# A four-batch attention and MLP kernel: group 0 of the last layer moved behind the pair, its first product in seven half products

## The chip, the cores and the metric

The program runs on one core of one Trainium2 chip. The metric is the device time of one execution in microseconds (us). Engines are named as in the profile: PE (TensorE matmuls; PEld its weight loads), DVE (VectorE), ACT (ScalarE), POOL (GpSimd), SP (SyncE, which issues most DMAs).

## The reference

```python
def _attn_ref(q, k, v, tau):                    # q, k, v: 4 batches, 8 heads, 576 tokens, 64
    scores = scale * np.matmul(q, k.transpose(0, 1, 3, 2))
    thresh = np.max(scores, axis=-1, keepdims=True) - tau
    scores = np.where(scores >= thresh, scores, -1000000000.0)
    ...                                         # softmax, then attn @ v
def _moe_ref(x, w_in, w_out):                   # x: 2304 x 512, w_in: 512 x 2048, w_out: 2048 x 512
    h = x @ w_in
    g = np.where(h >= 1, h, np.where(h <= -1, 0.0, (h + 1) ** 2 / 4))
    return g @ w_out
def _moe2_ref(x, w_in, w_out):                  # the same sizes
    h = x @ w_in
    g = h * np.clip(h + 3.0, 0.0, 6.0) / 6.0
    return g @ w_out
```

The output is `_moe2_ref` of `_moe_ref` of the attention's output. The change lies in the second MLP, called layer two here.

## The kernel before

Every number is kept as a high and a low part (fp32r), so that a product of two numbers is three matmuls: high by high, high by low, low by high. The 2304 tokens stand in five groups: groups 0 to 3 are the first 512 tokens of each batch, group 4 the 256 tokens that are left of all four. The hidden size of 2048 is 16 blocks `f` of 128.

Layer two runs in three stages. **Plain groups** (`dense`, called on L1497 with `order3` = groups 3, 4, 0): for each `f` the first product (`em_h`, L716, 12 matmuls; line L725), the gate (ACT Relu L738, DVE L739), its high part (ACT `gh`, L742) and low part (POOL `gl`, L743), and two steps later the second product (`em_out`, 12 matmuls of 512 columns, L767). **The pair** (`unit`, L1344): groups 1 and 2 together, the first product by seven block products in place of eight (Strassen-Winograd over two halves of the contraction, two blocks `f` and the two groups). For each of the 8 pairs `p` of blocks there are seven products of 6 matmuls with 512 columns (L1362), copies of partial sums on ACT (L1383), sums on DVE (`C`, L1388), four gates (L1147, L1148), and group 1's second product for the pair of blocks before (`outs_of`, L1157; matmuls L1165). Group 2's gated values go to DRAM (`rr`). **The end** (L1420 on): group 2's second product by seven for eight, in matmuls of 256 columns (`out_product`, L1287; L1300), with its inputs loaded from `rr`, summed on DVE and split on ACT, POOL and DVE.

The products by seven need sums of weights. `combine` (L1457) makes those of w_in out of the split weights, on DVE (`ex` L1473, `ws`, `wz`), from the second plain group on; they go to DRAM (`sd`) and come back as `sw` (`fetch`, L1129). `weight_sums` (L1172) makes those of w_out beside the pair (`te`, `ts`, `tz`); they go to `td` and come back as `tw`. `prepare` (L1098) makes the sums of tokens for the pair beside the last plain group.

While group 3 runs, the weights of layer two are still being split (`split_a`, `split_b`, L118 to L152): per weight tile two ACT passes, three DVE passes on `w_c` (L133, L136, L142), a POOL add (L144), the high part on ACT (L146) and the low part on POOL (L148). There are two `w_c` buffers. `ahead3` (L1485) calls this for each step. Each engine runs its queue in order; the order of the queues is fixed when the program is built.

Of the kernel before, what the change touches and what calls it, by code (L numbers as in the profile page):

```python
# [18 lines left out]
def kernel(  # L19
# [50 lines left out]
    td = [dram.tile([128, 2, 2, 512], F32R, name=f"td{p}") for p in range(KF // 2)]  # L70
    rd2 = [dram.tile([128, MAIN], F32, name=f"rr{f}") for f in range(KF)]
    xd, x2p, x2d = ([dram.tile([128, KD, n], F32, name=f"{nm}{w}") for w, n in enumerate(WIDE)]
# [67 lines left out]
    def split_b(kind, m, f):  # L140
# [6 lines left out]
        after(x, pins["S"])  # L147
        x = G.tensor_tensor(out=lo, in0=f32(c), in1=f32(hi), op=ALU.subtract)  # L148
# [918 lines left out]
    order3 = [NB - 1, NB, 0]  # L1067
# [30 lines left out]
    def prepare(step):  # L1098

        for c in range(2):  # L1100
# [6 lines left out]
            if step == 1:  # L1107
                part(0, c, b11)
                minus(t1, b12, b11)
            elif step == 2:  # L1110
                part(1, c, b21)
                minus(t2, b22, t1)
                minus(b12, b22, b12)
            elif step == 3:
                part(2, c, t2)
                minus(b11, t2, b21)
            elif step == 4:
                part(3, c, b12)
                part(4, c, b11)
            elif step == 5:  # L1120
                part(5, c, t1)
            elif step == 6:
                part(6, c, b22)

# [47 lines left out]
    def weight_sums():  # L1172

        for p in range(KF // 2):
            ex = []
            for f in (2 * p, 2 * p + 1):
                hi, lo = wsp["o", 1, f]
                t = wide["x"].tile([128, 512], F32, tag="xh3", name="te", bufs=2)
# [4 lines left out]
            s, u = (wide["x"].tile([128, 512], F32, tag="xl3", name="ts", bufs=2) for _ in range(2))  # L1183
            minus(s[:, 0:256], b12, b11)
            minus(s[:, 256:512], b22, s[:, 0:256])
            yield
            minus(u[:, 0:256], b22, b12)
            minus(u[:, 256:512], s[:, 256:512], b21)
            yield
            zs = []  # L1190
            for t in (s, u):
                z = stage.tile([128, 2, 512], F32R, tag="w_raw", name="tz", bufs=RAW)
                paced(S.activation(out=z[:, 0, :], in_=t, func=ACTF.Copy), "S")
                zs.append((t, z))
            yield
            for n, (t, z) in enumerate(zs):
                minus(z[:, 1, :], t, f32(z[:, 0, :]))
                nc.sync.dma_start(out=f32(td[p])[:, n], in_=f32(z))
                yield

    tw = {}

    def fetch_sum(n):

        p, x = divmod(n, 4)
        if p < 3:
            t = wide["x"].tile([128, 512], F32R, tag=RING[len(ring) % 6], name="tw", bufs=2)
            ring.append(t)
        else:
            t = place_of((n - 12) // 2, "hl"[n % 2], F32R, "tw")  # L1210
# [5 lines left out]
    def load_pair(p):  # L1216

        if p in (0, 2):
            rr[p] = [wide["p"].tile([128, MAIN], F32, tag="xst", name="r2", bufs=3) for _ in range(2)]
        elif p in (1, 3):  # L1220
            rr[p] = [wide["p"].tile([128, MAIN], F32, tag="xst", name="r2", bufs=3),
                     wide["t"].tile([128, MAIN], F32, tag="t0", name="r2")]
# [4 lines left out]
        for t, f in zip(rr[p], (2 * p, 2 * p + 1)):  # L1227
            nc.sync.dma_start(out=t, in_=rd2[f])
# [15 lines left out]
    def high_pair(p):  # L1244

        if p % 3 == 0:
            d = [[wide["x"].tile([128, 512], F32R, tag=tag, name="gt", bufs=2) for _ in range(2)]
                 for tag in ("xh3", "xl3")]
# [3 lines left out]
        elif p % 3 == 1:  # L1252
            d = [halves(f, "gt") for f in range(10, 14)]
        else:
            d = [(ringed("gh", F32R), ringed("gl", F32R)) for _ in range(4)]
        d[0] = [t[:, 0:256] for t in d[0]]
# [30 lines left out]
    def out_product(p, k, behind=None):  # L1287
# [5 lines left out]
        else:  # L1293
            n = {5: 0, 2: 1, 3: 2, 4: 3}[k]
# [14 lines left out]
    def out_sums(k):  # L1309
# [7 lines left out]
        def result(i, n, x, y, sign=1.0):  # L1317
            o = wide["p"].tile([128, 512], F32, tag="io", name="ob", bufs=3)
            scaled(o, x, y, sign)
            for m, q in enumerate((nc.sync, nc.scalar)):  # L1320
                q.dma_start(out=rows_of(G2, 2 * i + m)[:, n * 256:n * 256 + 256], in_=o[:, m * 256:m * 256 + 256])
# [22 lines left out]
    def unit():  # L1344

        accs, gg = {}, {}
        sums_of = weight_sums()
        last_p = KF // 2 - 1
        for p in range(KF // 2):

            def product(k, role, first=True):
# [4 lines left out]
                if first:  # L1356
                    banks[role] = bank(f"Q{(p + role) % 4}")
                y = 0
                for c in range(2):
                    xh, xl = combos[c, x]  # L1360
                    for l, r in ((0, xh), (0, xl), (1, xh)):
# [3 lines left out]
                        if p == last_p:  # L1365
                            after(mm, pins["T"])
                        pins["T"] = mm
                if p < last_p:
                    fetch(p + 1, w)
                    next(sums_of, 0)  # L1370
                else:
                    if k:
                        fetch_sum(4 + k)
                    {1: sum_pair, 2: high_pair, 3: low_pair}.get(k, lambda _: 0)(0)
                    if k == 3:
                        load_pair(2)
                return banks[role]

            banks = {}

            def copy(name, x):
                t = wide["p"].tile([128, MAIN], F32, tag="pb", name=name, bufs=KD)
                S.activation(out=t, in_=x, func=ACTF.Copy)  # L1383
                return t

            def add(name, x, y, op=ALU.add):
                t = place_of(14 + (name[2] == "2"), "hl"[name[1] == "2"], F32, name)
                V.tensor_tensor(out=t, in0=x, in1=y, op=op)  # L1388
                return t

            def outs(i):
                if p:
                    for f in (2 * p - 2, 2 * p - 1):
                        outs_of(G1, accs, i, f, gg[f], pins["T"] if p == last_p else None)

            def store(r, f):
                nc.sync.dma_start(out=rd2[f], in_=r)

            if p == last_p:
# [128 lines left out]
```

## Time and profile before

| | us |
|---|---|
| median of 3 runs | 1100.63 (1100.17 to 1101.37) |
| the profiled execution, its own time | 1102.58 |
| its span, first to last instruction | 1100.8 |
| PE busy | 1067.0 (97%) |
| DVE, ACT, POOL busy | 740.7, 656.6, 454.0 |

PE's granted clock was 0.992 on average. Matmuls are pipelined, so the time of one is longer than the distance from its start to the next one's start; the distance is what a matmul costs in a full stream. Layer two's plain groups run from about 710 us, the pair from about 930 us, the end from about 1046 us.

### The profile page before, as it was taken

Reading aid. Unit: us, or ns where it says so; the run is one execution under the profiler, and the core shown is the slowest. Engines: PE = TensorE matmul, PEld = TensorE weight load, DVE = VectorE, ACT = ScalarE, POOL = GpSimd, SP = SyncE. Lnnn points to the kernel's source line nnn. Section 1 sums busy time; section 2 is a strip of 40 time slices with the busy share of each in tenths; the row PEclk is TensorE's granted clock in tenths of the full one; section 3 lists DMA queues with packets and bytes.
Section 4 is the critical chain, followed back from the end, with each engine's and each line's share of the span. In section 5 each row is a group of like instructions: output and inputs, shape, how many; then the busy total and the mean of one; then the engine's idle time right before and its main releaser. Section 6 shows DMA issues by size and latency. Waiting matters only on the chain.

```text
span 1100.8 us, 18826 instructions
## 1 busy us (share of the span) xinstructions
PE 1067.0 (97%) x6658; PEld 882.2 (80%) x6658; DVE 740.7 (67%) x1432; ACT 656.6 (60%) x1304; POOL 454.0 (41%) x390
## 2 busy tenths in 40 slices
PE   7988889999999999999999999999999999999998
PEld 5555567777888888888889888888898888888888
DVE  5899887976676757256536755458565655778766
ACT  5777887776766767465556666645544333544542
POOL 0233667742222322146636665567723222211242
PEclk9999889999999999999999999999999999999999
DMA  6454446233222221015323555655244412877891
GB/s 170 117 98 101 117 118 149 64 75 88 70 66 66 45 61 44 30 50 172 94 73 125 164 178 164 212 169 154 77 154 151 136 58 67 269 259 250 279 348 39
DMA packets 178190, 140.97 MB, mean 128 GB/s; under 512 B 103088, under 2 KB 144304, under 8 KB 178096
## 3 DMA queue, kind: packets, MB, share of 16 engines
q1 hardware_dynamic: 176176, 138.95, 43.3%
q8 instruction: 52, 0.85, 0.3%
q10 hardware_dynamic: 1920, 0.82, 0.3%
q14 instruction: 42, 0.34, 0.1%
HBM read 93.00 MB, written 46.73 MB: 127 GB/s over the span
## 4 chain that ended last, share of the span: by engine, by line
PE 83%; DVE 8%; DMA 3%; ACT 2%; issue 1%; POOL 1%; SPq 1%; DVEq 0%; ACTq 0%; POOLq 0%
PE Q L725 27%; PE P L767 20%; PE Q L787 7%; PE Q L1362 6%; PE Q L482 6%; PE P L381 5%; PE Q L295 4%; PE P L1165 3%; DVE p L396 3%; DVE p L418 2%; PE P L1300 2%; PE Q L1300 1%; DMA tw<-td 1%; DVE xl L706 1%; SPq L234 1%
## 5 line engine op out<-in xcount | busy, mean ns | idle before, releaser
L743 POOL TENSOR_TENSOR gl<-r,gh 128x256 fp32r<-128x256 f32 (+1 forms) x158 | 167.1, 1058 | 324.6 <-ACT gh L742 312.2
L725 PE MATMUL Q<-xh,wih 128*128 128x256 f32 (+1 forms) x632 | 211.8, 335 | 2.6 <-DVE r L736 2.3
L725 PE MATMUL Q<-xl,wih 128*128 128x256 f32 (+1 forms) x632 | 207.3, 328 | 0.0
L725 PE MATMUL Q<-xh,wil 128*128 128x256 f32 (+1 forms) x632 | 207.2, 328 | 0.0
L736 DVE SCALAR_TENSOR_TENSOR r<-r,Q 128x256 f32<-128x256 f32 (+1 forms) x110 | 54.8, 498 | 124.6 <-ACT r L735 120.8
L418 DVE SCALAR_TENSOR_TENSOR p<-p,th,e 128x576 f32<-128x576 f32 x144 | 127.7, 909 | 15.8 <-ACT e L409 10.0
L725 PEld LDWEIGHTS Q<-xh,wih 128*128 128x128 f32 x632 | 120.1, 190 | 21.0 <-DVE r L736 4.1
L742 ACT ACTIVATE gh<-r 128x256 fp32r<-128x256 f32 (+1 forms) x158 | 79.6, 504 | 86.6 <-DVE r L736 31.1
L409 ACT ACTIVATE e<-p,nm 128x576 f32<-128x576 f32 x144 | 109.4, 775 | 36.2 <-DVE p L396 35.3
L725 PEld LDWEIGHTS Q<-xl,wih 128*128 128x128 f32 x632 | 120.2, 190 | 10.9
L725 PEld LDWEIGHTS Q<-xh,wil 128*128 128x128 f32 x632 | 120.1, 190 | 10.3
L295 PE MATMUL Q<-ident,p 128*128 128x128 f32 x656 | 107.3, 281 | 12.8 <-ACT Gf L446 9.7
L295 PEld LDWEIGHTS Q<-ident,p 128*128 128x128 f32 x656 | 74.0, 141 | 42.4 <-ACT Gf L446 16.1
L144 POOL TENSOR_TENSOR w_c<-w_c,w_raw 128x512 int32<-128x512 int32 x64 | 89.5, 1399 | 39.9 <-DVE w_c L142 20.6
L381 PE MATMUL P<-kt,qt 64*128 64x288 f32 (+2 forms) x508 | 82.8, 412 | 10.1 <-DVE p L396 8.1
L446 ACT ACTIVATE Gf<-Q 128x512 f32<-128x512 f32 x128 | 74.2, 595 | 15.8 <-PE Q L295 15.1
L1362 PE MATMUL Q<-xw,sw 128*128 128x512 f32 x336 | 81.0, 390 | 0.0
L396 DVE TENSOR_SCALAR_CACHE_REDUCE p<-P 128x576 f32<-128x576 f32 x90 | 65.2, 751 | 18.9 <-PE Q L295 11.9
L734 ACT ACTIVATE r<-Q,half 128x256 f32<-128x256 f32 (+1 forms) x110 | 58.5, 534 | 32.2 <-PE Q L725 25.3
L787 PE MATMUL Q<-gh,woh 128*128 128x256 f32 x240 | 75.3, 314 | 1.4 <-DVE ob L800 1.4
L1362 PEld LDWEIGHTS Q<-xw,sw 128*128 128x128 f32 x336 | 62.9, 188 | 13.6 <-DVE C L1388 0.7
L482 PE MATMUL Q<-Gf,vn 128*64 128x320 f32 (+1 forms) x512 | 72.8, 423 | 0.1
(199 smaller groups left out, 2454.5 us busy)
## 6 DMA issues: line engine op xcount, KB each, us to landing
w_raw<-in_moe_w_in_dram SPq DMA_DIRECT2D x32, 512.0 KB
w_raw<-in_moe_w_out_dram SPq DMA_DIRECT2D x32, 512.0 KB
sw<-sd SPq DMA_DIRECT2D x56, 256.0 KB
sd<-wz SPq DMA_DIRECT2D x32, 256.0 KB
td<-tz SPq DMA_DIRECT2D x16, 512.0 KB
tw<-td SPq DMA_DIRECT2D x32, 256.0 KB
vn<-in_v_dram SPq DMA_DIRECT2D x32, 128.0 KB
x2p<-ob SPq DMA_DIRECT2D x16, 256.0 KB
```

The costliest lines, as they stand in the source:

```text
L144: x = G.tensor_tensor(out=c.bitcast(I32), in0=c.bitcast(I32), in1=r, op=ALU.add)
L295: x = T.transpose(out, in_, ident)
L381: mm = T.matmul(o, a[j][r, cs], w[j][r, k0:k0 + HS], start=(n == 0), stop=(n == len(terms) - 1), skip_group_check=True)
L396: reads(V.tensor_scalar(out=p[:, x], in0=s[:, :, 0:HS], scalar1=taus[:, 3:4] if j >= JR else -1.0, scalar2=3e38, op0=ALU.mult, op1=ALU.min ...
L409: pins["S"] = S.activation(out=e, in_=p[:, x], func=ACTF.Exp, bias=nm[:, x:x + 1], scale=-1.0)
L418: pins["M"] = V.scalar_tensor_tensor(out=p[:, x], in0=p[:, x], scalar=th[:, x:x + 1], in1=e, op0=ALU.is_le, op1=ALU.mult, accum_out=zt[j][ ...
L482: mm = T.matmul(o[h * D:(h + 1) * D], vn[j % 2][:, c, h, :], f[:, h, c] if c < 4 else t, start=(c == 0), stop=(c == 4), skip_group_check=True)
L725: mm = T.matmul(h, l[:, kk * 128:(kk + 1) * 128], r, start=(x == 0), stop=(x == 3 * KD - 1))
L743: y = G.tensor_tensor(out=gl, in0=r, in1=f32(gh), op=ALU.subtract)
L767: T.matmul(a, l, r, start=(first and x == 0), stop=(last and x == 2))
L787: mm = T.matmul(o, l, r, start=(f == fs[0] and x == 0 and i == 0), stop=(f == fs[-1] and x == 2 and i == 1), skip_group_check=True)
L1362: mm = T.matmul(banks[role], t[:, l, c, :], r, start=(first and y == 0), stop=(y == 5), skip_group_check=True)
```

## The change

Group 0 leaves `order3`. After the pair a second unit runs for group 0 alone: its two halves of 256 tokens take the places that groups 1 and 2 have in the pair, so that its first product is seven products of 6 matmuls with 256 columns per pair of blocks. Beside it runs group 2's second product, now in the plain form (its gated values come back from `rr` in `again`). The end is the same as before, but for group 0 (its gated values go through a new DRAM buffer `rs`). Group 1 is as before, beside the pair.

`combine` no longer adds high and low: the exact weight is written to a new DRAM buffer `ed` from ACT's queue in `split_b`, and read back. Sums for 4 of the 8 pairs of blocks (`first_sums`) are now made while group 3 runs, in steps `n` = 4 to 17 of `ahead3`; the other 4 beside the pair. The token sums of the pair (`prepare`) move to group 4's steps, those of group 0's halves (`small_step`) to the last two rounds of the pair. The sums of w_out for 2 of 8 pairs of blocks are made beside the pair and go through `td`; those for the other 6 are made beside the second unit and stay on chip.

```diff
-    order3 = [NB - 1, NB, 0]
+    order3 = [NB - 1, NB]
+    G0 = 0
...
+        if (kind, m) == ("i", 1):
+            nc.scalar.dma_start(out=ed[f], in_=f32(c))
...
+    def small_load(c):
+        raw2[c] = [wide["p"].tile([128, MAIN], F32, tag="xst", name="ty", bufs=3) for _ in range(3)]
+        for t, kk in zip(raw2[c], (c, 2 + c)):
+            nc.sync.dma_start(out=t, in_=x2d[G0][:, kk, :])
...
+    def unit(second, between):
+        n = 256 if second else MAIN
+        xs_of = combos2 if second else combos
...
-                if p < last_p:
-                    fetch(p + 1, w)
-                    next(sums_of, 0)
+                if p < last_p:
+                    fetch(p + 1, w)
+                elif not second:
+                    fetch(0, w)
+                between(p, turn[0])
...
+    def beside_first(p, k):
+        next(late, 0)
+        if 3 <= p < last_p - 1:
+            next(early_t, 0)
...
+    def beside_second(p, k):
+        if k in (2, 4):
+            again(2 * p + (k == 4))
+        if p < last_p:
+            if k < 7:
+                next(sums_of, 0)
...
-        ex = []
-        for n, f in enumerate((f0, f1)):
-            hi, lo = wsp["i", 1, f]
-            t = wide["p"].tile([128, 512], F32, tag="pb", name="ex", bufs=KD)
-            paced(V.tensor_tensor(out=t, in0=f32(hi), in1=f32(lo), op=ALU.add), "V")
+        for t, f in zip(ex, (2 * p, 2 * p + 1)):
+            nc.sync.dma_start(out=t, in_=ed[f])
...
+        if n < KF:
+            plain(n)
+        if n >= 4:
+            next(first_sums, 0)
+        if 6 <= n < KF:
+            next(first_sums, 0)
...
-    unit()
+    unit(False, beside_first)
+    unit(True, beside_second)
+    last_group()
```

In DVE's queue, two steps of group 3 late in the weight splitting before (`r` is the gate, the three `w_c` rows are one weight tile):

```order
L739 SCALAR_TENSOR_TENSOR r_9191<-r_9191,Q0_9178 128x512
L133 TENSOR_SCALAR w_c_9212<-w_c_9212 128x512
L136 TENSOR_SCALAR w_c_9212<-w_c_9212 128x512
L142 SCALAR_TENSOR_TENSOR w_c_9212<-w_raw_9086,w_c_9212 128x512
L739 SCALAR_TENSOR_TENSOR r_9236<-r_9236,Q1_9223 128x512
```

and the same place in the changed kernel, blocks 9 to 11 (lines are four or two higher; `ws` and `wz` are sums and low parts of w_in):

```order
L743 SCALAR_TENSOR_TENSOR r_9295<-r_9295,Q0_9282 128x512
L144 SCALAR_TENSOR_TENSOR w_c_9261<-w_raw_9106,w_c_9261 128x512
L1096 TENSOR_TENSOR wz_9277<-ws_9223,wz_9276 128x512
L1096 TENSOR_TENSOR wz_9280<-ws_9224,wz_9279 128x512
L135 TENSOR_SCALAR w_c_9316<-w_c_9316 128x512
L138 TENSOR_SCALAR w_c_9316<-w_c_9316 128x512
L144 SCALAR_TENSOR_TENSOR w_c_9316<-w_raw_9161,w_c_9316 128x512
L743 SCALAR_TENSOR_TENSOR r_9349<-r_9349,Q1_9336 128x512
L1578 TENSOR_TENSOR ws_9385<-ex_9382 128x256
L135 TENSOR_SCALAR w_c_9370<-w_c_9370 128x512
L1096 TENSOR_TENSOR ws_9385<-ws_9385,ex_9381 128x256
L138 TENSOR_SCALAR w_c_9370<-w_c_9370 128x512
```

Two `ws` or `wz` rows now stand in each step; from the gate of block 6 to that of block 13 there are 8 `ws` and 6 `wz`.

On PE, group 0's first product before, one block `f`, with its first rows:

```order
L725 MATMUL Q_10477<-xh,wih_8848 128x512
L725 MATMUL Q_10477<-xl,wih_8848 128x512
L725 MATMUL Q_10477<-xh,wil_8849 128x512
L725 MATMUL Q_10477<-xh,wih_8848 128x512
L725 MATMUL Q_10477<-xl,wih_8848 128x512
```

and now, a round of the second unit (L1439 the products by seven, L1221 group 2's second product):

```order
L1439 MATMUL Q_11600<-xz,sw 128x256 x6
L1439 MATMUL Q_11613<-xz,sw 128x256 x6
L1221 MATMUL P_11489<-woh_7808,gh 128x512
L1221 MATMUL P_11489<-wol_7809,gh 128x512
L1221 MATMUL P_11489<-woh_7808,gl 128x512
...
L1439 MATMUL Q_11600<-xz,sw 128x256 x6
L1439 MATMUL Q_11653<-xz,sw 128x256 x6
```

The 192 matmuls of 512 columns (12 for each of 16 blocks) become 336 of 256 columns (6 by 7 by 8); no other kind of matmul changes its number.

In DVE's queue, a round of the pair before, from its first sum of w_out (`te`) on:

```order
L1179 TENSOR_TENSOR te_11332<-woh11_8985,wol11_8986 128x512
L1388 TENSOR_TENSOR C11_11349<-Q1_11336,p1_11334 128x512
L1091 TENSOR_TENSOR ts_11345<-te_11321 128x256
L1091 TENSOR_TENSOR ts_11345<-te_11332,ts_11345 128x256
L1148 SCALAR_TENSOR_TENSOR r_11351<-r_11351,C11_11349 128x512
L1091 TENSOR_TENSOR ts_11346<-te_11332,te_11321 128x256
L1091 TENSOR_TENSOR ts_11346<-ts_11345,te_11332 128x256
L1091 TENSOR_TENSOR tz_11390<-ts_11345,tz_11390 128x512
```

and a round of the second unit now (L1416 the sums `C`, L1467 the gates, both of 256 columns; the low parts `tw` in place of `tz`):

```order
L1416 TENSOR_TENSOR C12_11733<-Q1_11697,U2_11651 128x256
L1467 SCALAR_TENSOR_TENSOR C12_11733<-C12_11733 128x256
L1243 TENSOR_TENSOR te_11747<-woh6_8404,wol6_8405 128x512
L1243 TENSOR_TENSOR te_11760<-woh7_8536,wol7_8537 128x512
L1416 TENSOR_TENSOR C11_11762<-Q0_11751,p1_11749 128x256
L1467 SCALAR_TENSOR_TENSOR C11_11762<-C11_11762 128x256
L1096 TENSOR_TENSOR te_11747<-te_11747 128x256
L1096 TENSOR_TENSOR te_11747<-te_11760,te_11747 128x256
L1096 TENSOR_TENSOR te_11760<-te_11760,te_11747 128x256
L1096 TENSOR_TENSOR te_11760<-te_11760 128x256
L1416 TENSOR_TENSOR C21_11830<-U3_11828,Q1_11791 128x256
L1416 TENSOR_TENSOR C22_11845<-Q2_11835,U3_11828 128x256
```

The work on w_out's sums in a round is the same; the sums `C` and gates are half as wide, and the gates of C12 and C11 stand right behind their sums.

## Rows read from the trace of the kernel before

**Rows 1.** The page's first part: busy time, share of the span, instructions.
```profile
PE 1067.0 (97%) x6658; PEld 882.2 (80%) x6658; DVE 740.7 (67%) x1432; ACT 656.6 (60%) x1304; POOL 454.0 (41%) x390
```

**Rows 2.** Busy time by stretch: PE, PEld, DVE, ACT, POOL, clock, DMA share, GB/s.
```profile
740.00:797.00 57.00, 57.00 (x252) 46.77 (x251) 39.70 (x42) 31.19 (x53) 44.06 (x33) 1.00 0.40 123
930.00:1046.00 116.00, 116.00 (x513) 95.85 (x511) 84.84 (x129) 54.04 (x90) 23.86 (x18) 1.00 0.77 257
1040.00:1060.00 20.00, 19.32 (x112) 16.63 (x111) 15.19 (x21) 10.13 (x19) 10.68 (x9) 1.00 1.01 354
```

**Rows 3.** Timeline of PE (start, us, instruction): streams of 512 and 256 columns.
```profile
849.30 0.39 PE L725 MATMUL Q<-xh,wih 128*128 128x512 f32 x1
...
852.02 0.39 PE L767 MATMUL P<-woh,gh 128*128 128x512 f32 x1
...
1074.69 1.60 PE L1300 MATMUL P<-tw,gz 128*128 128x256 f32 x12
1076.13 0.28 PE L1300 MATMUL P<-woh,gz 128*128 128x256 f32 x1
```

**Rows 4.** Timeline of PE where the pair gives way to the end.
```profile
1057.59 0.28 PE L1300 MATMUL Q<-wol,gh 128*128 128x256 f32 x1
1058.40 0.38 PE L1300 MATMUL Q<-woh,gl 128*128 128x256 f32 x1 [0.53 <-POOL gl L1267]
...
1058.86 0.28 PE L1300 MATMUL Q<-woh,gl 128*128 128x256 f32 x1
1059.29 0.50 PE L1165 MATMUL P<-woh,gh 128*128 128x512 f32 x1 [0.15 <-DVE ob L830]
```

**Rows 5.** Timeline of POOL late in the weight splitting.
```profile
759.46 1.48 POOL L743 TENSOR_TENSOR gl<-r,gh 128x512 fp32r<-128x512 f32 x1
...
770.15 1.30 POOL L148 TENSOR_TENSOR wol<-w_c,woh 128x512 fp32r<-128x512 f32 x1 [0.75 <-ACT woh L146]
771.41 1.74 POOL L743 TENSOR_TENSOR gl<-r,gh 128x512 fp32r<-128x512 f32 x1
773.12 1.30 POOL L144 TENSOR_TENSOR w_c<-w_c,w_raw 128x512 int32<-128x512 int32 x1
775.17 1.30 POOL L148 TENSOR_TENSOR wil<-w_c,wih 128x512 fp32r<-128x512 f32 x1 [0.74 <-ACT wih L146]
```

**Rows 6.** Timeline of DVE in the same stretch.
```profile
759.83 1.40 DVE L136 TENSOR_SCALAR w_c<-w_c 128x512 uint32<-128x512 uint32 x1
...
769.72 0.43 DVE L136 TENSOR_SCALAR w_c<-w_c 128x512 uint32<-128x512 uint32 x1
770.19 1.81 DVE L142 SCALAR_TENSOR_TENSOR w_c<-w_raw,w_c 128x512 uint32<-128x512 uint32 x1
```

**Rows 7.** Timeline of PE in the same stretch.
```profile
772.62 0.39 PE L767 MATMUL P<-woh,gh 128*128 128x512 f32 x1
772.84 0.39 PE L767 MATMUL P<-wol,gh 128*128 128x512 f32 x1
773.21 0.50 PE L767 MATMUL P<-woh,gl 128*128 128x512 f32 x1
```

**Rows 8.** DVE's groups, 797 to 1060 us: count | busy us, mean ns | idle before.
```profile
L1148 DVE SCALAR_TENSOR_TENSOR r<-r,C 128x512 f32<-128x512 f32 x32 | 23.4, 735 | 10.6 <-ACT r L1147 10.3
L1091 DVE TENSOR_TENSOR tz<-ts,tz 128x512 fp32r<-128x512 f32 x16 | 14.3, 907 | 2.1 <-ACT tz L1193 1.8
L1179 DVE TENSOR_TENSOR te<-woh,wol 128x512 f32<-128x512 f32 x16 | 13.8, 890 | 0.0
...
L1473 DVE TENSOR_TENSOR ex<-wih,wil 128x512 f32<-128x512 f32 x16 | 10.3, 682 | 0.0
L1091 DVE TENSOR_TENSOR ts<-te 128x256 f32<-128x256 f32 x16 | 8.4, 552 | 0.0
...
L739 DVE SCALAR_TENSOR_TENSOR r<-r,Q 128x256 f32<-128x256 f32 x16 | 6.7, 417 | 15.6 <-ACT r L738 15.6
...
L1091 DVE TENSOR_TENSOR ws<-ws,ex 128x256 f32<-128x256 f32 x8 | 3.3, 413 | 0.0
```

**Rows 9.** ACT's groups in the same stretch.
```profile
L738 ACT ACTIVATE r<-Q,three 128x256 f32<-128x256 f32 x16 | 7.5, 471 | 13.4 <-PE Q L725 10.0 <-POOL gl L743 3.4
```

More of the change, by code (lines that the diff above doesn't have):

```diff
@@ new lines, in sink @@
+            def sink(t, row, col):
+                if second:
+                    r = t[:, 256:512]
+                    S.activation(out=r, in_=t[:, 0:256], func=ACTF.Relu, bias=three)
+                    pins["V"] = V.scalar_tensor_tensor(out=r, in0=r, scalar=6.0, in1=t[:, 0:256],
+                                                       op0=ALU.min, op1=ALU.mult)
+                    nc.sync.dma_start(out=rd3[(f0, f1)[row]][:, 256 * col:256 * col + 256], in_=r)
+                elif col:
+                    nc.sync.dma_start(out=rd2[(f0, f1)[row]], in_=gate(t))
+                else:
+                    gg[(f0, f1)[row]] = parts(gate(t))
@@ new lines, in unit @@
+            p1 = copy("p1", product(0, 0), n)
+            sink(add("C11", product(1, 1), p1, n), 0, 0)
+            outs(0)
+            u2 = copy("U2", product(2, 0, False), n)
+            c21 = product(4, 2)
+            outs(1)
+            u3 = copy("U3", product(3, 0, False), n)
+            sink(add("C21", u3, c21, n, ALU.subtract), 1, 0)
+            sink(add("C22", product(5, 3), u3, n), 1, 1)
+            outs(2)
+            outs(3)
+            sink(add("C12", product(6, 3, False), u2, n), 0, 1)
@@ new lines, in unit, with again @@
+            between(p, 7)
+    hh = {}
+    def again(f):
+        r = ringed("r", F32)
+        nc.sync.dma_start(out=r, in_=rd2[f])
+        hh[f] = parts(r)
+    def beside_first(p, k):
+        next(late, 0)
+        if 3 <= p < last_p - 1:
+            next(early_t, 0)
+        if p == last_p - 2 and k == 7:
+            small_load(0)
+        elif p == last_p - 1 and k < 6:
+            small_step(k + 1, 0)
+        elif p == last_p - 1 and k == 7:
+            small_load(1)
+        elif p == last_p and 0 < k < 7:
+            small_step(k, 1)
@@ L1481, in combine, with in_turn @@
         minus(s2, s1, a11)
+        yield
         minus(s3, a11, a21)
         minus(s4, a12, s2)
+        yield
+        d = []
+        for n, t in enumerate(s):
+            if early:
+                z = [wide["t"].tile([128, 512], F32R, tag=f"t{2 * n + x}", name="wz") for x in range(2)]
+            else:
+                z = stage.tile([128, 2, 512], F32R, tag="w_raw", name="wz", bufs=RAW)
+                z = [z[:, 0, :], z[:, 1, :]]
+            paced(S.activation(out=z[0], in_=t, func=ACTF.Copy), "S")
+            d.append((z, t))
+        yield
+        for n, (z, t) in enumerate(d):
+            minus(z[1], t, f32(z[0]))
+            for x in range(2):
+                nc.sync.dma_start(out=sd[p][:, 4 + 2 * n:6 + 2 * n, x, :],
+                                  in_=f32(z[x]).rearrange("p (s n) -> p s n", s=2))
+            yield
+    EARLY = 4
+    def in_turn(ps, early):
+        for p in ps:
+            yield from combine(p, early)
+    first_sums = in_turn(range(EARLY), True)
+    late = in_turn(range(EARLY, KF // 2), False)
+    early_t, sums_of = weight_sums((6, 7)), weight_sums(range(6))
     def ahead3(n, g, f):
```

248 lines of the change are left out of this document (139 added, 109 removed).

## The prediction

> **What bounds the kernel now.** I read the page's first part, then busy time by stretch, then PE's timeline, and only where PE slips the timelines of the engines that feed it. PE is busy for 1067.0 of 1100.8 us [rows 1], and in the two stretches of layer two that the change touches most it has no idle time at all: 57.00 of 57.00 and 116.00 of 116.00 us [rows 2]. So the time of layer two is the number of matmuls by the distance from one start to the next, plus the few places where PE slips. The distance is not the duration in the record. Twelve matmuls of 512 columns lie between the starts at 849.30 and 852.02, so 2.72 / 12 = 0.2267 us each, though each record says 0.39; twelve of 256 columns lie between 1074.69 and 1076.13, so 0.120 each [rows 3]. Half the columns cost a little more than half the time (0.1133).
>
> PE slips at two kinds of place. One is where the pair gives way to the end: from 1057.59 to 1058.40 lie 0.81 us where 0.12 is due, and from 1058.86 to 1059.29 lie 0.43 [rows 4]. The first waits for POOL's low part, in a stretch where the DMA engines stand at 1.01 of their time and 354 GB/s [rows 2]. The other is the weight splitting beside group 3. There POOL works 44.06 of 57 us [rows 2] and runs just in time: its low part starts at 771.41, takes 1.74 and so ends at 773.15 [rows 5]; the matmul that reads it starts at 773.21, 0.37 behind the one before it instead of 0.227 [rows 7].
>
> **The sum starts** from the profiled execution's own 1102.58, which is 1.95 above the median of 1100.63. I take 1.95 off at the end.
>
> **PE's work: -3.2.** The order shows that 192 matmuls of 512 columns go (192 x 0.2267 = 43.5 us) and 336 of 256 columns come (336 x 0.120 = 40.3). Group 2's second product turns plain as group 0's turns into one by seven, so these two trade places. All of it lies on the path, since PE has no idle time there.
>
> **The step from the pair to the end: -1.0.** The two slips above are 0.69 + 0.31 = 1.0 us. In the changed kernel the end's first sums rest on group 0's values, which are read back a round and more earlier, and 24 of 32 loads of `tw` are gone since those weights stay on chip. The crowd of transfers that made POOL late is thus thinned out. If something else is late there, the term is 0; I see nothing that is: the output's tail is the same.
>
> **Weight splitting with sums beside it: +1.6 (0 to +4.1).** Between the gates of blocks 6 and 13 DVE gets 8 more additions of 256 columns and 6 of 512, each with two inputs in SBUF. DVE has the time (39.70 of 57 us busy [rows 2]; the new work is 8 x 0.413 + 6 x 0.907 = 8.7 us [rows 8]). The question is POOL, for the two engines slow each other. DVE's pass L136 takes 0.43 alone and 1.40 beside POOL [rows 6]. POOL's operation takes 1.30 alone, 1.48 beside a short pass of DVE's and 1.74 beside the longer L142, which itself stretches to 1.81 [rows 5, 6]. So an addition of 256 columns may cost POOL 0.18 and one of 512 columns 0.44: 8 x 0.18 + 6 x 0.44 = 4.1 if each meets an operation of POOL's. It is 0 if they fall into POOL's waits for ACT, 0.74 or 0.75 in each step [rows 5]. Between the ends goes what POOL has to spare: its step is 1.74 + 1.30 + 0.74 + 1.30 = 5.08 us [rows 5], PE's is 24 x 0.2267 = 5.44. That is 0.36 a step, 2.5 us over the 7 steps, and 4.1 - 2.5 = 1.6. POOL is late already when the stage begins, so I don't take less. ACT gets 6 passes and one DMA issue per weight tile; it is busy for 31.19 of 57 us [rows 2], so these are free, and the `w_c` buffer that the DMA reads is held a little longer, which I count within the same bounds.
>
> The Trainium skill ("SBUF — State Buffer", section "Who interferes with whom") speaks against this part of the change: it says that a DVE instruction with two SBUF inputs contends with GpSimd's reads, through a port that one of them holds and the other is fully blocked from. The sizes of the rows, 0.44 lost beside an operation that takes 0.69 alone, are those of sharing and not of a full block; if it were full, the rival on the lock below would hold.
>
> **The second unit: +0.8 (0 to +6.9).** A round of it is 42 x 0.120 + 24 x 0.2267 = 10.48 us of PE. DVE has to do in that time, in rounds 0 to 5 [rows 8]: two `te` of 0.890 (1.78); four half-width sums between 0.413 and 0.552, nearer the second (2.06); two low parts of 0.907 (1.81); four `C` that read PSUM, like L739 at 256 columns 0.417 (1.67); four gates of 256 columns between 0.413 and the 0.735 that 512 columns take, about 0.45 (1.8). That is 9.1 us. Then there are waits: in the pair the gate L1148 waited 10.6 us in 32 times, 0.33 each, for ACT [rows 8]. Now the gates of C12 and C11 stand right behind the sums that ACT must pass through Relu first; that pass is 0.471 at 256 columns [rows 9], with the two handovers about 0.67 (an estimate). Two such waits and 0.33 for the other two gates give 9.1 + 1.34 + 0.33 = 10.8 against 10.48. Over 6 rounds DVE falls 1.9 behind, of which PE bears about 1.1 without waiting: products 0 and 2 are 6 x 0.120 + 6 x 0.2267 = 2.08 apart and the copy between takes about half of that. Left is 0.8. If the waits are 0.33 all round, a round is 10.4 and nothing shows; if all four are 0.67, it is 11.8, and 6 x 1.32 - 1.0 = 6.9 shows.
>
> **At nothing:** the token sums of the pair beside group 4 and those of group 0 in the pair's last two rounds, since DVE is busy for 84.84 of 116 us in the pair [rows 2] and no longer makes `ex` (16 x 0.682 = 10.3 us less [rows 8]) nor `te`, `ts`, `tz` for six of eight pairs of blocks there. SP's loads for them are more in number, but the pair moves 257 GB/s at 0.77 of the DMA engines' time [rows 2], and each load is issued some 10 us ahead of its use. If that cover were gone, a late `sw` would cost PE its own delay once a round.
>
> **The sum:** 1102.58 - 3.2 - 1.0 + 1.6 + 0.8 = 1100.8, less 1.95: **1098.8 us**. A change of less than 0.2% (2.2 us) is about what a measurement of this kernel can't tell from none, so faster begins below 1098.4 and slower above 1102.8. My forecast stands just inside "same", own range 1097.4 to 1100.4.
>
> **The rivals.**
>
> *All of it is hidden.* The sums in group 3 fall into POOL's waits, DVE keeps up in the second unit: 1102.58 - 4.2 - 1.95 = 1096.4. For it: PE's idle time is nil in the whole stretch although POOL is busy for 77% of it. Against: the low part that came 0.06 us before its use [rows 5, 7].
>
> *Weight splitting pays in full.* Every addition meets POOL, and POOL's spare time is eaten by its being late at the start: +4.1 for +1.6, 1101.3. Against: POOL's step is shorter than PE's.
>
> *DVE sets the pace of the second unit (slower).* One mechanism: gates that wait behind ACT in a queue that has no time left. It decides once a round of DVE's is over 10.48 us by more than about 0.2, and at 11.8 the time is 1098.8 - 0.8 + 6.9 = 1104.9. For it: 9.1 us of plain work is 87% of PE's round, and the queue is in order, so a gate that waits keeps `C` and the sums of the next blocks. Against: in the pair the same order of queue waited 0.33 a gate and PE had no idle time.
>
> *A full lock between DVE and POOL.* Each addition stops POOL for the whole of its time: 8 x 0.413 + 6 x 0.682 (what `ex`, two inputs and 512 columns, took [rows 8]) = 7.4, less the 2.5 to spare = 4.9 in place of 1.6: 1102.1. The row of 1.74, +0.44 beside a DVE pass that takes 0.69 alone, speaks against it.
>
> That the change doesn't do what it says can be left out: the order has the 336 matmuls in place of the 192.
>
> **Chances.** The forecast 0.45; all hidden 0.22; weight splitting in full 0.16; DVE in the second unit 0.13; the lock 0.04. Of the forecast's own range a little under half lies below 1098.4. Faster: 0.20 + 0.22 = 0.42. Same: 0.25 + 0.16 + 0.04 = 0.45. Slower: 0.13. The range goes from just under the hidden case, 1096.2, up to 1103.2, so that it leaves out most of the slower case and the end of the hidden one, under 2 in 10.
>
> **What the profile after would show.** In PE's timeline, streams of 256 columns 0.120 apart in group 0's first product. At the step to the end, no gap over 0.3. In group 3, POOL's low parts at 1.5 to 1.75 and a sum of slips of PE between about 745 and 795 us of some 1.6; if it is near nothing, the sums were hidden; over 4, they were not. In the second unit (some 84 us before the end) PE's idle time near 1 us, and DVE busy for about 9 of each 10.5 us with most idle before the gates; if PE waits for DVE in each round, the slower rival holds. Wrong I would be altogether if PE waited on a DMA in the pair (a late `sw` or `ex`), for which I have no term.

## The result and the profile after

| | kernel before | changed kernel |
|---|---|---|
| median, us | 1100.83 (6 runs) | 1111.38 (6 runs, 1108.09 to 1114.89) |
| ratio | 1 | 1.0098, 95% interval 1.0078 to 1.0118 |
| profiled execution, own time | 1102.58 | 1111.60 |

The changed kernel is slower by 10.6 us, where 1.8 us less was forecast and 1103.2 was the range's upper end. The first part of the page of the changed kernel answers to [rows 1]:

```profile
PE 1068.9 (96%) x6802; PEld 886.4 (80%) x6802; DVE 752.0 (68%) x1482; ACT 669.8 (60%) x1354; POOL 451.3 (41%) x390
```

It shows the 144 matmuls more and some 11 and 13 us more of work on DVE and ACT, but not where the time went. Busy time by stretch (PE, PEld, DVE, ACT, POOL, clock, DMA share, GB/s), as in [rows 2], shows where to look:

```profile
740.00:797.00 57.00, 52.64 (x227) 41.69 (x225) 50.59 (x55) 31.61 (x54) 42.03 (x30) 1.00 0.75 237
976.00:1058.00 82.00, 79.84 (x496) 71.56 (x496) 61.01 (x120) 42.99 (x93) 26.63 (x21) 1.00 0.91 305
1040.00:1060.00 20.00, 19.51 (x124) 17.42 (x124) 10.79 (x21) 9.83 (x22) 8.93 (x8) 1.00 0.87 269
```

In the first stretch PE had no idle time before and now lacks 4.4 of 57 us, DVE's work has gone from 39.70 to 50.59 us, and the DMA engines from 0.40 to 0.75 of their time.

I call a slip what a matmul's distance to the next one has over 0.2267 or 0.120 us, counted from 0.15 us on. PE's timeline of layer two gives this account of the two profiled executions:

| place in the changed kernel | slip before | slip after |
|---|---|---|
| group 3's stage, 755 to 805 us | 0 | 5.35 |
| group 4, 819 us | 0 | 1.10 |
| pair's first rounds, 868 us | 0 | 0.17 |
| pair to second unit, 979 us | - | 1.83 |
| second unit's last round, 1053 us | - | 0.65 |
| step to the end, 1070 us | 1.00 | 0.97 |
| slips under 0.15, all layer two | 1.2 | 2.5 |
| matmuls, 336 x 0.120 - 192 x 0.2267 | | -3.2 |

The last row rests on the stream of 256 columns, which is as dense in the new unit as in [rows 3], 13 matmuls in 1.55 us:

```profile
973.80 1.72 PE L1439 MATMUL Q<-xz,sw 128*128 128x256 f32 x13
975.35 0.40 PE L1221 MATMUL P<-woh,gh 128*128 128x512 f32 x1
```

The sum is 10.1 - 1.0 + 1.3 - 3.2 = +7.2 us. Another slip of 0.55 stands at 665 us, in layer one. About 1.1 us lie before 476 us, in the attention, whose end varied between 472.9 and 476.2 us over the profiled executions of all kernels here. That is 8.9 of the 9.0 us between the two profiled executions.

**Group 3's stage.** PE waits for POOL's low part `gl`, as in [rows 7] but far longer:

```profile
774.79 0.39 PE L771 MATMUL P<-woh,gh 128*128 128x512 f32 x1
775.02 0.39 PE L771 MATMUL P<-wol,gh 128*128 128x512 f32 x1
777.93 0.50 PE L771 MATMUL P<-woh,gl 128*128 128x512 f32 x1 [2.52 <-POOL gl L747]
```

Two causes run into this one slip. The first is on ACT, whose timeline shows the pass into `w_c` (L134) waiting for the transfer that still reads that buffer:

```profile
759.86 0.35 ACTq L151 DMA_DIRECT2D ed<-w_c  x1
...
765.03 0.67 ACT L134 ACTIVATE w_c<-w_raw 128x512 f32<-128x512 f32 x1 [3.09 <-DMA ed<-w_c]
765.60 0.67 ACT L742 ACTIVATE r<-Q,three 128x512 f32<-128x512 f32 x1
766.17 0.62 ACT L148 ACTIVATE woh<-w_c 128x512 fp32r<-128x512 f32 x1
...
777.45 0.66 ACT L134 ACTIVATE w_c<-w_raw 128x512 f32<-128x512 f32 x1 [2.97 <-DMA ed<-w_c]
```

The transfer is issued at 759.86 and lets ACT go at 765.03, 5.2 us later; ACT had stood ready since 761.94 (765.03 less the wait of 3.09). A gate (L742) and a high part of a weight (L148) are queued behind the waiting pass. Of all waits for `ed` in the trace this is the largest group (us, times):

```profile
  ACT w_c L134: 22.5, 12
```

Only three of the twelve waits lie in this stage (3.09, 2.97 and 3.49 us). Nine lie before it, between 590 and 745 us, and there PE has just the one slip of 0.55.

The second cause is on DVE. Three of its additions for the sums, of 256 columns:

```profile
760.62 1.53 DVE L1578 TENSOR_TENSOR ws<-ex 128x256 f32<-128x256 f32 x1
...
768.37 1.51 DVE L1096 TENSOR_TENSOR ws<-ex,ws 128x256 f32<-128x256 f32 x1
...
783.77 1.52 DVE L1096 TENSOR_TENSOR ws<-ws,ex 128x256 f32<-128x256 f32 x1
```

and the operations of POOL that run beside them, with the two ahead of the slip at 775 us:

```profile
760.57 1.31 POOL L152 TENSOR_TENSOR wil<-w_c,wih 128x512 fp32r<-128x512 f32 x1 [0.75 <-ACT wih L148]
...
768.13 1.47 POOL L747 TENSOR_TENSOR gl<-r,gh 128x512 fp32r<-128x512 f32 x1
...
774.54 1.67 POOL L146 TENSOR_TENSOR w_c<-w_c,w_raw 128x512 int32<-128x512 int32 x1 [0.63 <-DVE w_c L144]
776.17 1.71 POOL L747 TENSOR_TENSOR gl<-r,gh 128x512 fp32r<-128x512 f32 x1
...
783.53 1.48 POOL L152 TENSOR_TENSOR wil<-w_c,wih 128x512 fp32r<-128x512 f32 x1
```

An addition that [rows 8] has at 0.413 takes 1.5 us. In all three cases POOL started first (0.05 to 0.24 us ahead), lost at most 0.18 itself, and DVE ended 0.27 or 0.28 us after POOL. DVE stood for nearly the whole of POOL's operation. Of the 8 `ws` and 4 `wz` that start between 757 and 796 us, eight began while an operation of POOL's was running: the six of 256 columns ended 0.27 to 0.29 us after it, the two of 512 columns 0.55. The four others took 0.41 or 0.68 us. Together the twelve take 13.8 us; by [rows 8] they were priced at 6.9. So DVE's passes on `w_c` come late, POOL's add (L146, 0.63 waiting for DVE) after them, and `gl` behind that add.

**Edges.** At 819 and 979 us PE waits for DVE to empty a PSUM bank (`ob`), which stands in DVE's queue behind other work. At 819 us that is a sum of tokens, which waited 2.23 us and was let go, by the profile, by the last of the sums' writes (`sd<-wz`). At 979 us it is what these rows of DVE, and the matmul that waits for it on PE, show:

```profile
977.21 1.33 DVE L1204 SCALAR_TENSOR_TENSOR r<-r,C 128x512 f32<-128x512 f32 x1 [0.83 <-ACT r L1203]
978.46 1.28 DVE L1243 TENSOR_TENSOR te<-woh,wol 128x512 f32<-128x512 f32 x2
979.67 0.41 DVE L1467 SCALAR_TENSOR_TENSOR C<-C 128x256 f32<-128x256 f32 x1
980.00 0.41 DVE L1096 TENSOR_TENSOR te<-te 128x256 f32<-128x256 f32 x1
980.34 1.27 DVE L834 TENSOR_SCALAR ob<-P 128x512 f32<-128x512 f32 x2
...
981.07 0.50 PE L1221 MATMUL P<-woh,gh 128*128 128x512 f32 x1 [1.67 <-DVE ob L834]
```

At the step to the end, where [rows 4] had its slips, DVE waits for a load, and an `ob` stands behind it:

```profile
1069.26 0.76 DVE L1296 TENSOR_TENSOR gs<-r 128x256 f32<-128x256 f32 x1 [4.08 <-DMA r<-rs]
1069.94 0.41 DVE L1096 TENSOR_TENSOR gs<-r 128x256 f32<-128x256 f32 x1
1070.27 0.68 DVE L834 TENSOR_SCALAR ob<-P 128x512 f32<-128x512 f32 x1
```

That load was held up in SP's queue (here its order in the program, and then its times):

```
L1469 DMA rs14_138<-C12_12423 128x256
L1286 DMA r2_12719<-rs14_138 128x512
L1286 DMA r_12450<-rs6_130 128x512
L1286 DMA r_12451<-rs7_131 128x512
```

```profile
1061.90 0.38 SPq L1469 DMA_DIRECT2D rs<-C  x1
1064.99 1.74 SPq L1286 DMA_DIRECT2D r<-rs  x4
```

Block 14's load waits for the last write of block 14, 2.7 us, and the loads of blocks 6 and 7, which the end needs first, come behind it.

### The profile page after: what moved, and what is told of

The parts are those of the page before. It is cut to its first block, busy times and chain, and to the rows that moved or that the text cites. A ratio compares the mean times of both kernels' runs of the same rounds, so it can differ in the third digit from the quotient of the medians.

```text
span 1109.8 us, 19519 instructions
## 1 busy us (share of the span) xinstructions
PE 1068.9 (96%) x6802; PEld 886.4 (80%) x6802; DVE 752.0 (68%) x1482; ACT 669.8 (60%) x1354; POOL 451.3 (41%) x390
## 4 chain that ended last, share of the span: by engine, by line
PE 71%; DVE 12%; DMA 6%; ACT 4%; issue 4%; POOL 2%; SPq 1%; DVEq 0%; ACTq 0%; POOLq 0%
PE Q L729 17%; PE P L771 10%; PE Q L1439 10%; PE P L1221 7%; PE Q L791 7%; PE Q L486 6%; PE P L385 6%; PE Q L299 5%; DMA ed<-w_c 4%; DVE p L400 2%; DVE p L422 2%; PE P L1362 2%; PE Q L1362 1%; DVE w_c L144 1%; DVE w_c L138 1%
## 5 line engine op out<-in xcount | busy, mean ns | idle before, releaser
L747 POOL TENSOR_TENSOR gl<-r,gh 128x256 fp32r<-128x256 f32 (+1 forms) x142 | 145.0, 1022 | 258.5 <-ACT gh L746 240.3
L729 PE MATMUL Q<-xh,wih 128*128 128x256 f32 (+1 forms) x568 | 187.0, 329 | 2.5 <-DVE r L740 2.4
L729 PE MATMUL Q<-xl,wih 128*128 128x256 f32 (+1 forms) x568 | 182.4, 321 | 0.0
L729 PE MATMUL Q<-xh,wil 128*128 128x256 f32 (+1 forms) x568 | 182.2, 321 | 0.0
L422 DVE SCALAR_TENSOR_TENSOR p<-p,th,e 128x576 f32<-128x576 f32 x144 | 124.5, 886 | 16.2 <-ACT e L413 10.4
L729 PEld LDWEIGHTS Q<-xh,wih 128*128 128x128 f32 x568 | 108.1, 190 | 18.5 <-DVE r L740 4.0
L729 PEld LDWEIGHTS Q<-xl,wih 128*128 128x128 f32 x568 | 108.1, 190 | 8.4
L729 PEld LDWEIGHTS Q<-xh,wil 128*128 128x128 f32 x568 | 108.0, 190 | 8.1
L746 ACT ACTIVATE gh<-r 128x256 fp32r<-128x256 f32 (+1 forms) x142 | 69.4, 490 | 67.0 <-DVE r L740 36.2
L146 POOL TENSOR_TENSOR w_c<-w_c,w_raw 128x512 int32<-128x512 int32 x64 | 89.6, 1400 | 48.2 <-DVE w_c L144 25.1
L1210 POOL TENSOR_TENSOR gl<-r,gh 128x512 fp32r<-128x512 f32 x32 | 43.3, 1360 | 150.6 <-ACT gh L1209 146.5
L1439 PE MATMUL Q<-xw,sw 128*128 128x512 f32 x336 | 81.8, 389 | 0.0
```

Of the source, the lines that this page charges most:

```text
L146: x = G.tensor_tensor(out=c.bitcast(I32), in0=c.bitcast(I32), in1=r, op=ALU.add)
L422: pins["M"] = V.scalar_tensor_tensor(out=p[:, x], in0=p[:, x], scalar=th[:, x:x + 1], in1=e, op0=ALU.is_le, op1=ALU.mult, accum_out=zt[j][ ...
L729: mm = T.matmul(h, l[:, kk * 128:(kk + 1) * 128], r, start=(x == 0), stop=(x == 3 * KD - 1))
L747: y = G.tensor_tensor(out=gl, in0=r, in1=f32(gh), op=ALU.subtract)
L1439: mm = T.matmul(banks[role], t[:, l, c, :], r, start=(first and y == 0), stop=(y == 5), skip_group_check=True)
```

## The experiments

Each run is one kernel. Slips are those of its one profiled execution; the median is set beside that of the kernel before on the same chip. The order of the queues is laid out anew when a kernel is built, so that an edit also moves neighbours.

**The exact weight's transfer, from another source.**

```diff
-            nc.scalar.dma_start(out=ed[f], in_=f32(c))
+            nc.scalar.dma_start(out=ed[f], in_=f32(hi))
```

> The exact weight's transfer to DRAM (16 of 256 KB) reads the high part's tile and not the buffer w_c; so the sums lack the weights' low part, all transfers and all work on the engines stay. Theory A (ACT stands still at the next Abs into w_c until the transfer has read the buffer, 12 times, 22.5 us in the changed kernel, and the high parts queued behind it on ACT come late, then POOL's low parts): those waits go, PE's slips between 755 and 805 us fall from 5.2 us to under 0.7, and the time from 1111.4 to about 1106.5. Theory B (the sums on DVE slow POOL through a shared port): the slips stay over 4 us and the time over 1110.

Measured: 1109.36 (before 1100.67, ratio 1.0084, interval 1.0072 to 1.0096). ACT waits for the transfer no more, but 4.6 us of slips stay in group 3's stage; 1.4 of them are PE's clock, which fell after the longest wait (last section). The held buffer alone isn't the cause. By the times, what letting it go saves here can't be told from nothing: the interval overlaps that of the changed kernel.

**No early sums.** `combine` skips reads, additions, high and low parts for the early pairs and sends the weights' own parts to DRAM instead.

```diff
+        if early:
+            yield
...
+                    nc.sync.dma_start(out=sd[p][:, 4 + 2 * n:6 + 2 * n, x, :],
+                                      in_=f32(wsp["i", 1, 2 * p + n][x]).rearrange("p (s n) -> p s n", s=2))
```

> The sums of w_in of the four early pairs of blocks are left out: no reads of the exact weight for them, no additions on DVE and no high parts on ACT; in their place the weights' own parts go to DRAM, as many bytes. The exact weight is still written out of w_c. Theory A (the buffer held by the transfer): ACT's waits for it stay near 20 us, PE's slips between 755 and 805 us stay over 3 us, time about 1108.5 to 1110. Theory B (the sums slow POOL): the slips fall under 1 us and the time to about 1105. Under both the slip of 1.1 us at 819 us, where DVE waits for token loads that follow the sums' last writes, goes.

Measured: 1107.47 (before 1100.67, ratio 1.0063, interval 1.0050 to 1.0077). Slips of 2.9 us stay there, without a fall of the clock; ACT waits 13.3 us in 10 times, and the slip at 819 us is gone. So neither theory alone holds.

**Both out.**

> Both edits to group 3's stage at once: the early pairs' sums of w_in left out (the weights' own parts go to DRAM in their place), and the exact weight's transfer reads the high part's tile, not w_c. Each alone left slips of PE there (2.9 us without the sums, 4.6 without the held buffer, against 5.4 with both). Theory (the two together are all that this stage lost): the slips between 755 and 805 us fall under 0.7 and the one at 819 us is gone; 1111.4 - 5.4 - 0.7 - 1.1 = about 1104.2. Rival (the order in which the queues were laid out, or the transfers' number, costs it): over 2 us of slips remain, 1106 or more.

Measured: 1102.68 (before 1101.23, ratio 1.0014, interval 1.0003 to 1.0026). Not one slip between 500 and 850 us but 0.41 at 556. Busy time from 757 to 800 us (columns as above) of the kernel before, the changed kernel, the run without early sums and this one:

```profile
757.00:800.00 43.00, 43.00 (x195) 35.43 (x194) 28.78 (x32) 21.85 (x38) 30.78 (x23) 1.00 0.38 117
757.00:800.00 43.00, 38.64 (x165) 30.08 (x164) 39.02 (x45) 22.13 (x38) 29.57 (x21) 1.00 0.74 231
757.00:800.00 43.00, 40.95 (x174) 31.89 (x173) 24.31 (x28) 20.88 (x36) 29.36 (x23) 1.00 0.48 151
757.00:800.00 43.00, 43.00 (x197) 35.80 (x197) 26.77 (x27) 20.87 (x35) 31.92 (x24) 1.00 0.52 170
```

Together the two are all that the stage lost, and the slip at 819 us is gone, as it was already when only the sums were left out. It is 1.5 us under the expected 1104.2; in this profiled execution the attention ended 2.6 us earlier than in that of the changed kernel, which no edit here explains. Left were 2.16 at the second unit, 0.66 in its last round and 2.12 at the step to the end.

**The held buffer alone, in the kernel before.**

```diff
         x = S.activation(out=hi, in_=f32(c), func=ACTF.Copy)
         after(x, pins["S"])
+        if (kind, m) == ("i", 1):
+            nc.scalar.dma_start(out=ed[f], in_=f32(c))
```

> The kernel before, with one thing added: after each high part of w_in ACT's queue sends the exact weight from w_c to DRAM, where nothing reads it. Theory (the held buffer costs by itself): ACT waits for the transfer in about ten tiles, PE slips 2 to 3 us between 745 and 800 us, 1100.7 to about 1103.3. Rival (the held buffer costs only where the sums have already made POOL late): within 0.7 us of 1100.7.

Measured: 1104.75 against 1101.23 (ratio 1.0030, interval 1.0018 to 1.0041). Slips of 2.9 us in the stage, as many as in the changed kernel without sums; ACT waits 16.7 us in 10 times. A transfer that nobody reads costs this kernel some 3.5 us:

```profile
757.00:800.00 43.00, 41.17 (x179) 32.38 (x179) 23.89 (x28) 21.33 (x36) 29.17 (x22) 1.00 0.41 129
```

**What of the sums costs.** As the first run, without DVE's part of the early sums.

```diff
+        if early:
...
+            for n, t in enumerate(ex):
+                z = wide["t"].tile([128, 512], F32R, tag=f"t{2 * n}", name="wz")
+                paced(S.activation(out=z, in_=t, func=ACTF.Copy), "S")
...
+            return
```

> As the run with the transfer from the high part's tile (1109.4, slips of 4.6 us in group 3's stage, no held buffer), and DVE's additions and low parts for the four early pairs are left out; their reads, ACT's passes to high parts and the writes stay (the read tile in place of the sum, the high part sent twice). Theory (DVE's own work is what the sums cost: 14 operations that take 1 to 1.5 us each beside POOL, on an engine that then has nothing to spare): slips under 0.7 us, about 1103.5. Rival (ACT's passes, or the reads and writes on the transfer engines): slips over 2.5 us, 1107 or more.

Measured: 1103.71 (before 1101.00, ratio 1.0024, interval 1.0013 to 1.0035). No slip in the stage. Busy time from 757 to 800 us of the first run (transfer from the high part, sums whole), and then of this one:

```profile
757.00:800.00 43.00, 40.11 (x169) 32.40 (x168) 39.41 (x42) 23.09 (x41) 32.23 (x24) 0.96 0.68 214
```

```profile
757.00:800.00 43.00, 43.00 (x195) 35.41 (x194) 26.06 (x28) 24.47 (x43) 31.03 (x24) 1.00 0.74 231
```

ACT has as much to do and the DMA engines more; DVE's 39.41 of 43 us fall to 26.06. DVE's own operations are what the sums cost. POOL's busy time hardly differs. Whether they cost it by being stretched beside POOL or would do so at 0.41 and 0.68 us each too, no run tells apart.

**Two tries for another buffer.** The first gave w_in's tiles one buffer of their own, the second (a whole computation too) only the result of POOL's add:

```diff
-        c = stage.tile([128, 512], U32, tag="w_c", name="w_c", bufs=2)
+        if (kind, m) == ("i", 1) and "t" in wide:
+            c = wide["t"].tile([128, 512], U32, tag="t4", name="w_c")
+        else:
+            c = stage.tile([128, 512], U32, tag="w_c", name="w_c", bufs=2)
```

> The tiles of w_in are split in a third buffer, which nothing else uses then; the transfer of the exact weight, the sums and the result stay whole. Theory A (ACT waits for the buffer): the waits go and the time falls to about 1106.5, as with the transfer from the high part. Theory B (port): no change, 1110 to 1112. A rival within A, that the transfers themselves crowd out others, would leave this one as slow as now.

Measured: 1124.68, ratio 1.0216, slower than the change itself. ACT's waits fell to 3.2 us in 3 times, but the queues were laid out otherwise and PE slipped at new places: 4.2 us at 669 us, where it waited for ACT's high parts of tokens (`xh`), and 2.2 at 806. The run decides nothing about the buffer.

```diff
+        d = c
+        if (kind, m) == ("i", 1):
+            c = wide["t"].tile([128, 512], U32, tag="t4", name="w_e")
-        x = G.tensor_tensor(out=c.bitcast(I32), in0=c.bitcast(I32), in1=r, op=ALU.add)
+        x = G.tensor_tensor(out=c.bitcast(I32), in0=d.bitcast(I32), in1=r, op=ALU.add)
```

> POOL's add of a w_in tile writes the exact weight into a tile of its own (idle at that time), and the transfer reads that; w_c comes free after the add. All sums are whole. Theory (held buffer and sums in one stage, each enough for most of the loss): ACT's waits for the transfer go, slips of 3 to 5 us stay in group 3's stage because of the sums, as with the transfer from the high part: 1108.5 to 1110. Rival (the buffer is the cause, and what the transfer from the high part still lost came from elsewhere): below 1106.

Measured: 1110.45 (before 1100.56, ratio 1.0091). No waits of ACT for the transfer, 4.9 us of slips, 1.4 of them the clock's, as in the first run and without leaving anything out.

**The edges.**

```diff
-            if k < 7:
+            if 0 < p and k < 7:
                 next(sums_of, 0)
```

> Beside the second unit the sums of w_out begin a round later (rounds 1 to 6 in place of 0 to 6, of which the last was partly empty); nothing else changes. Theory: PE's slip of 1.83 us at 979 us, where group 1's last output waits in DVE's queue behind two te of 0.64 and a gate, goes: 1111.4 to about 1109.6. Rival: the gates and sums C of the new unit make the output late all the same; the slip stays over 1 us and the time within 1110.5 to 1111.5.

Measured: 1111.70. The slip at 979 us fell to 0.29 as expected, and yet nothing was gained: 0.73 came up in the next round and 2.53 in place of 0.97 at the step to the end. The next run adds this to it:

```diff
-            nc.sync.dma_start(out=t, in_=rd3[f])
+            x = nc.sync.dma_start(out=t, in_=rd3[f])
+            if p == 3:
+                pins["rs"] = x
+            elif p == last_p:
+                after(x, pins["rs"])
```

> The sums of w_out begin a round later, as in the run on that alone, and on SP the loads of the end's last pair of blocks (14, 15) come behind those of its fourth (6, 7), where block 14's load, which waits for the last write out of its buffer, held them up. Theory (the slip that the later sums saved came back at the step to the end, 2.53 in place of 0.97, because of that load): the slip at the step falls under 1.0 us, and the time from 1111.7 to about 1109.8. Rival (the transfers of the second unit, 0.91 of the DMA engines' time, are what is late): the slip stays over 2 us, 1111 to 1112.

Measured: 1109.09. No slip is left at the step to the end, with the transfers unchanged. The load that waited ahead of others in SP's queue was the cause there, and gave back what the later sums saved.

**All places out.**

> All the places at once: the early pairs' sums of w_in left out, the exact weight's transfer from the high part's tile, the sums of w_out a round later, and the loads of the end's last pair behind those of its fourth. If the account is whole, what is left is the change in PE's matmuls and a slip or two under 1.1 us: 1102.7 less 2.2 at 968 us and 2.1 at the step to the end, plus up to 1.1 in the unit's second round, 1098.5 to 1100, below the kernel before (1101.2). Rival (the 336 matmuls of 256 columns cost as much as the 192 of 512, so that the unit itself saves nothing): 1101 or more.

Measured: 1099.96 against 1100.56, ratio 0.9996, interval 0.9987 to 1.0005. From the attention's end to PE's last matmul it is 619.8 us, before 621.4. The account closes: -3.2 for the matmuls, 2.3 of slips left (0.36 and 0.70 in the unit's first two rounds, 0.46 in its last, 0.58 after the step, 0.17) against 1.0 before, 0.4 more of small ones, -1.5. So even with the early sums, the held buffer and the edges' worst out, what the change saves can't be told from nothing in the time.

**Whole computations with less of it.** Two early pairs in place of four, one piece in a step:

```diff
-    EARLY = 4
+    EARLY = 2
...
-        if 6 <= n < KF:
-            next(first_sums, 0)
```

> Two pairs of blocks in place of four get their sums of w_in while group 3 runs, one piece in each step instead of two; the other six are made beside the pair. Theory (what group 3's stage lost grows with the sums in it): slips there 1.5 to 3.5 us in place of 5.4, none at 819 us, DVE hides the two more pairs beside the pair; 1107.5 to 1109. Rival (a late sum then holds up PE in the pair): slips of over 1 us between 860 and 960 us, 1110 or more.

Measured: 1106.17 (before 1101.23, ratio 1.0045, interval 1.0033 to 1.0058); 3.0 us of slips in the stage, no wait in the pair over 0.17.

Then with the tile of its own and the two edits at the edges:

> The whole computation with four edits: the exact weight in a tile of its own, sums of w_in for two early pairs in place of four, the sums of w_out a round later, and the end's last loads behind its fourth pair's. Theory: 1106.2 (two early pairs) less 2.5 for the two edits behind the pair, less 1 to 3 for the held buffer: 1100.7 to 1102.7, no slower than the kernel before by more than 0.2%. Rival (the held buffer saves nothing as long as any sums are in the stage): 1103.5 or more.

Measured: 1103.58, ratio 1.0032 (1.0020 to 1.0045). The rival of this run is nearer: the two edits at the edges had saved 2.3 in the changed kernel (1111.38 to 1109.09), and 1106.17 less 2.3 is 1103.9, so what the own tile saved can't be told from nothing; 3.7 us of slips stayed in the stage.

The same, but two pieces in a step:

```diff
         if n >= 4:
             next(first_sums, 0)
+            next(first_sums, 0)
```

> As the run with four edits (1103.6; slips of 3.7 us in group 3's stage), but the pieces of the two early pairs stand two in a step, from step 4 to 9, in place of one in a step from 4 to 15, so that they end before block 10 of group 3. Theory (they cost where POOL has the late weights and the low parts of every block, from 757 us on): slips there under 1.5 us, 1100.7 to 1102. Rival (they cost the same wherever they stand beside the splitting): slips of 3 us or more between 730 and 800 us, 1103 or more.

Measured: 1105.05 (before 1101.00, ratio 1.0038, interval 1.0024 to 1.0052); 4.9 us of slips, from 760 us on. Standing earlier gained nothing. But the last of the pieces ran until 767.5 us and not, as expected, until 757, and 1.8 of the 4.9 lie at 780 us and later, behind the last piece; no run explains these. No whole version beats the kernel before.

## Why the prediction was wrong

**PE's work, -3.2: right.** The 256-column stream is 0.120 apart in the second unit too; with everything else out, the account from the attention's end closes with this term. The time of that run by itself, 0.9996 with an interval from 0.9987 to 1.0005, doesn't show it.

**Weight splitting, +1.6 (0 to 4.1): wrong, and the largest miss.** It measured 5.4, and 1.1 more at 819 us, where a sum of tokens waited for the sums' last writes. That is 4.9 over the term; the second unit was 1.7 over its own, the step to the end 1.0, and the slips under 0.15 us, for which there was no term, came to 1.3. So this term alone didn't turn the sign: with all of it out the kernel still measured 1.0014 (1.0003 to 1.0026). Two things failed in it.
- "The `w_c` buffer that the DMA reads is held a little longer, which I count within the same bounds" had no price. The buffer is one of two. In this stage ACT stood ready for its next pass into it 1.5 to 2.6 us after the transfer's issue, and the transfer let it go only after 5.0 to 5.5 us. What I should have asked is what is queued behind that pass on ACT: gates and high parts that POOL needs. Alone it costs 2.9 us of slips.
- "DVE has the time" was worked out from clean durations, and the collision was priced on POOL's side only. POOL gave up 0 to 0.18 us in those three cases, 0.44 at most; DVE paid 1.1 on an operation of 0.41. With that DVE is at 39.0 of the 43 us from 757 to 800, and every pass on `w_c` is late. The Trainium skill ("SBUF — State Buffer", section "Who interferes with whom") says that the order of issue decides who is blocked, and that the other waits for the whole instruction; the additions that end 0.27 to 0.29 us after POOL's operation agree with it. I used the rule with POOL as the loser, read POOL's loss of 0.44 as a sign of sharing, and gave the rival 0.04. [Rows 6] had the other side in plain sight: L136 at 1.40 and 0.43.

Both delay the same `gl`. Slips were 2.9 us with the held buffer alone, 4.6 or 4.9 with the sums alone, 5.4 with both and none with both out. The clock's fall makes up 1.4 us of the 4.6 and of the 4.9 and none of the 2.9 and 5.4; without it the two alone are 2.9 and 3.2 or 3.5. How much of each hides the other therefore stays open.

**The step to the end, -1.0: wrong.** The slips of [rows 4] went, and a load queued behind a waiting one gave 0.97. I had looked at how early loads could be issued and not at their order on SP, which the built program shows.

**The second unit, +0.8: nothing in its middle, more at its start.** From 990 to 1040 us PE has no idle time with DVE at 38.5 of 50 us (three quarters, not 9.1 of 10.5 and waits), so the rival of DVE as the bound there fell. The term's own sum had a slip too: it counts 0.33 once for two gates that its row prices at 0.33 each; with 0.66 a round comes to 11.1 and the term to about 2.6, further from a middle that cost nothing. The 1.83 at its start is an eviction (`ob`, DVE emptying a PSUM bank) behind `te` and gates, for which I had no term, and 0.65 came in its last round. When the 1.83 was taken away alone, it moved on to the step behind it.

**Of the rivals**, the lock was nearest, in size (4.9 for the 5.4) and in kind, but with POOL as the one that waits; weight splitting in full had 4.1 by POOL's losses as well. Neither had the held buffer. "All of it is hidden" held for no run that kept the early sums or the held buffer.

## What to carry to other kernels

A DMA that reads a buffer out of a rotation holds it until the transfer ends, here 5 us at 0.4 to 0.75 of the DMA engines' time; price it by what is queued on the engine that wants the buffer next. Where DVE and POOL work on SBUF side by side, cost the collision on both engines: here an addition of 256 columns that began during an operation of POOL's ended 0.27 to 0.29 us after it. Check the busier one's total with the stretched durations. When one slip goes and the time stays, look for the next place that waits on the same in-order queue.

## What the runs showed of the hardware

The clock of PE fell after a long wait in some runs and not in others. In the first experiment PE waited 2.86 us for `gl`; then seven distances of 0.426 to 0.43 us for 512 columns follow, that is 1.2 GHz, against 0.2267 at 2.4 GHz, and cost another 1.4 us:

```profile
775.06 0.50 PE L771 MATMUL P<-woh,gl 128*128 128x512 f32 x1 [2.86 <-POOL gl L747]
...
775.71 0.63 PE L771 MATMUL P<-wol,gh 128*128 128x512 f32 x1
776.14 0.63 PE L771 MATMUL P<-woh,gl 128*128 128x512 f32 x1
776.57 0.63 PE L771 MATMUL P<-woh,gh 128*128 128x512 f32 x1
...
779.03 0.39 PE L729 MATMUL Q<-xh,wih 128*128 128x512 f32 x1
```

The granted clock of the stretch from 770 to 780 us of that run was 0.83 (the third number from the end of the row):

```profile
770.00:780.00 10.00, 7.11 (x24) 5.08 (x23) 9.74 (x9) 5.35 (x9) 8.76 (x7) 0.83 0.78 236
```

In the changed kernel a wait of 2.52 us at a like place was followed by distances of 0.23, with no fall (granted clock 1.00 from 770 to 785 us). In the run with the tile of its own the fall came after shorter waits, 0.35 and 1.16 us within 2 us: seven distances of 0.43 again, and a granted clock of 0.57 from 777 to 781 us. So the length of the last wait doesn't decide it; what does was not tried.
